# More block products in an attention and token/channel mixer kernel: seven products instead of eight for the first channel product of batches 1 to 3 and for the second of all batches

## The chip, the cores and the metric

The kernel runs on one core of a Trainium2 chip. The metric is the time of one execution on the device in microseconds, the median of the runs of a kernel. Names of engines: PE is the matrix engine (PEld its weight loads), DVE the vector engine, ACT the scalar engine, POOL the general engine, which also issues the casting loads, and SP the engine that issues the other transfers. The kernel's matrix operands are bf16 and its sums fp32.

## The reference

The inputs are q, k and v of 4 batches, 8 heads, 768 positions and 64 channels per head, and four weights of the mixer. Attention keeps 4 sink positions and a window of 128:

```python
scores = scale * np.matmul(q, k.transpose(0, 1, 3, 2))
keep = (pos[None, :] < 4) | ((rel >= 0) & (rel < 128))
a = softmax(np.where(keep, scores, -1e9))
x = np.matmul(a, v)                       # heads side by side: (4, 768, 512)
h = np.maximum(x.T @ w_tok1, 0) @ w_tok2  # over positions, 768 -> 256 -> 768
u = x + h.T
h2 = np.maximum(u @ w_ch1, 0) @ w_ch2     # over channels, 512 -> 1536 -> 512
out = u + h2                              # fp32
```

## The kernel before

One program runs on all engines, with a written order. Heads go in 16 pairs (4 per batch). A pair is loaded as bf16 (`q_bf`, `k_bf`, `v_aug`), q and k are turned (by PE for pairs 0 to 7, by DMA from pair 8 on, `BY_DMA`), the scores of three groups of key tiles (`scores(p, g)`) go into one of two score banks `sc[0]` and `sc[1]`, ACT takes the exponential, DVE or POOL masks it (for the first four pairs PE adds a mask instead, but for one group), PE multiplies by v, and DVE normalizes into `x_sb`. Then come the token product (`mix_h`, `mix_u`), the transpose of u (`uT`), the first channel product with relu (`v1`, into `v1T`), the second channel product, the addition of u (`o_sb`), and the store.

- The first channel product is done in 24 units per batch: for each of 12 tiles of 128 hidden channels and each half of the 768 positions, four matmuls of 384 columns (channel tiles of u), then one eviction with relu on ACT or DVE (L157, L159).
- The second channel product of batches 1 to 3 (`BY_SEVEN = range(1, B)`) is a 2 x 2 block product done with seven products: sums S1 to S4 of blocks of v1T (`add_up`, L1025) and T1 to T4 of w_ch2 (`weight_sums`, L1260), and products accumulated in shared banks, between whose terms a bank is read out by DVE (`evict` in `products`, L1071). Batch 0 does it whole (`whole(st)`, 12 matmuls of 512 columns for each of six row tiles, evicted at L1153).
- [...] Two score tiles take two banks each; four are `mx` banks for all else; behind the first attention, the halves of `sc[1]` are also given out as `mx`.
- The score groups 1 and 2 of pairs 4 to 15 are computed by quarters of 64 rows when they come into `sc[0]`, and by halves when they come into `sc[1]`. Quarters leave out key and query blocks that are masked anyway, and what the bank held there before goes through the exponential and is multiplied by a mask of zeros and ones (L638).

The order of PE's units is the string `ORDERED`. A letter names a stream and a number the unit in it: t, m, s, o, g, h are the first attention and the tokens of batch 0; a the later attention, k the later tokens; c the first channel product; x and y the second one. A planner inside the kernel (`Plan`) walks along this order with costs for each operation and decides which engine does what else, and when. Operations that more than one engine can do go to the one that would end first; the loads are issued on POOL in the order of a list, at most eight outstanding. Each engine then runs its instructions in that order, and each instruction waits for the semaphores of what it needs.

```python
e = min(op.cost, key=lambda e: max(self.free[e], r) + op.cost[e])
```

Of the kernel before, what the change touches and what calls it, by code (L numbers as in the profile page):

```python
# [8 lines left out]

FP32 = mybir.dt.float32  # L10
# [6 lines left out]
def kernel(  # L17
# [43 lines left out]
    BY_SEVEN = range(1, B)  # L61
# [8 lines left out]
    mix_pool = ctx.enter_context(tc.tile_pool(name="mix", bufs=2))  # L70
    v1_pool = ctx.enter_context(tc.tile_pool(name="v1", bufs=1))
# [98 lines left out]
    ones = singles.tile([P, 4 * P], BF16)  # L170
# [11 lines left out]
    mask_main = singles.tile([P, 2, 2, 2, P], BF16)  # L182
    mask_first = singles.tile([P, 2, 2, 2, P], BF16)

    MASKED = -32768.0
    mask_add = singles.tile([P, 4, 2, P], BF16)
# [19 lines left out]
    NKB = 3  # L206
    kTb = [singles.tile([P, S], BF16, name=f"kT{n}") for n in range(NKB)]

# [9 lines left out]
    v_sink_f = singles.tile([P, NHP, 2, D1], FP32)  # L218
# [29 lines left out]
    SEM = 90.0  # L248
    PE_OUT = 190.0
# [10 lines left out]
    class Op:  # L260
        def __init__(self, cost, fn, deps=(), then=(), size=0.0, lag=None, loads=0, traffic=0.0):
# [7 lines left out]
            self.half = False  # L269
# [6 lines left out]
    class Plan:  # L276
        def __init__(self):
            self.free = {"PE": 0.0, "ACT": 0.0, "DVE": 0.0, "SP": 0.0, "POOL": 0.0}
            self.queue, self.landings = 0.0, []
            self.sent = 0.0  # L280
            self.half = False
            self.pending = []
            self.held = [()] * (2 * NSC + NMX)
            self.late = False

        def ready(self, op):
            t = 0.0
            for d in op.deps:
# [3 lines left out]
                t = max(t, d.done)  # L292
# [40 lines left out]
        def other(self):  # L333
            best = None
            queue = False
            for n, op in enumerate(self.pending):
# [6 lines left out]
                if r is not None and len(self.landings) + op.loads > LANES:  # L343
# [11 lines left out]
        def commit_pe(self, op, t):  # L355
# [6 lines left out]
            self.free["PE"] = t + op.cost["PE"] + SWITCH * (op.half != self.half)  # L362
            self.half = op.half
            op.done = self.free["PE"] + PE_OUT + SEM
# [30 lines left out]
    def unit(ns, fn, deps=(), need=None, then=(), half=False):  # L395
# [6 lines left out]
        op.half = half  # L402
        return op

    def burst(*pieces):
# [6 lines left out]
        def run():  # L412
            for p in pieces:
                p.fn()

        op = unit(
            sum(p.size for p in pieces), run, [d for p in pieces for d in p.deps], need,
            [t for p in pieces for t in p.then], half=True,
# [6 lines left out]
    def piece(ns, fn, deps, need, then, keys=()):  # L425
        op = Op({}, fn, deps, then, size=float(ns))
        op.need, op.keys = need, keys
        return op

    def joined(*units):  # L430
# [6 lines left out]
        for u in units:  # L437
# [6 lines left out]
            [t for u in units for t in u.then], half=units[0].half,  # L444
# [4 lines left out]
    def prepare(p):  # L449
# [23 lines left out]
        if p >= BY_DMA:  # L473
# [16 lines left out]
            def sinks_of(e):  # L490
# [5 lines left out]
                {"POOL": 300.0, "DVE": 300.0}, sinks_of, done["kT", p] + [("sk", p - NHP)],  # L496
# [3 lines left out]
        if parts == 2:  # L500
            cost = {"DVE": 540.0, "ACT": 500.0}
        else:
            cost = {"DVE": 950.0} if p < NHP else {"DVE": 950.0, "ACT": 900.0}
# [829 lines left out]
```

## Time and profile before

| | us |
|---|---|
| median of three runs | 205.46 |
| lowest and highest run | 204.59, 206.63 |
| span of the profiled execution, first to last instruction | 203.1 |
| PE busy | 191.1 |
| DVE busy | 130.5 |
| ACT busy | 105.8 |
| POOL busy, with issuing loads | 79.5 |

The profiled execution's own time beside its span isn't given; the median stands 2.4 us above the span. Busy time is the time in which at least one instruction of the engine ran; matmuls overlap, so the time of one matmul is read from the distance of the starts. The granted PE clock is full through nearly all of the span. One row of a timeline gives the start, the time, the engine, the line, the operation, the tile written and the tiles read, their shapes and the number of instructions, and in brackets how long the engine stood idle ahead of it and what ended that.

### The profile page before, as it was taken

Reading aid. Unit: us, or ns where it says so; the run is one execution under the profiler, and the core shown is the slowest. Engines: PE = TensorE matmul, PEld = TensorE weight load, DVE = VectorE, ACT = ScalarE, POOL = GpSimd, SP = SyncE. Lnnn points to the kernel's source line nnn. Section 1 sums busy time; section 2 is a strip of 40 time slices with the busy share of each in tenths; the row PEclk is TensorE's granted clock in tenths of the full one; section 3 lists DMA queues with packets and bytes.
Section 4 is the critical chain, followed back from the end, with each engine's and each line's share of the span. In section 5 each row is a group of like instructions: output and inputs, shape, how many; then the busy total and the mean of one; then the engine's idle time right before and its main releaser. Section 6 shows DMA issues by size and latency. Waiting matters only on the chain.

```text
span 203.1 us, 5055 instructions
## 1 busy us (share of the span) xinstructions
PE 191.1 (94%) x2098; PEld 129.9 (64%) x2107; DVE 130.5 (64%) x272; ACT 105.8 (52%) x189; POOL 79.5 (39%) x121
## 2 busy tenths in 40 slices
PE   6789997999999999999999999999999999999890
PEld 2435685566665564566677788756778886658780
DVE  4657656875978746576677888728657944235851
ACT  4598856878868214396774602677724002673000
POOL 6199869696696563766423050000000000003000
PEclk9999999999999999999999999999999999999997
DMA  5999999999999999999995275500002226100025
GB/s 172 274 283 181 166 185 186 163 170 206 165 152 146 123 184 209 162 157 200 169 131 104 49 87 155 210 0 3 15 14 53 46 62 245 38 0 3 0 101 209
DMA packets 92166, 26.28 MB, mean 129 GB/s; under 512 B 82416, under 2 KB 89072, under 8 KB 92144
## 3 DMA queue, kind: packets, MB, share of 16 engines
q0 software_dynamic: 67232, 11.80, 74.1%
q1 hardware_dynamic: 24912, 14.17, 31.9%
q8 instruction: 16, 0.26, 0.5%
q14 instruction: 6, 0.05, 0.1%
HBM read 26.75 MB, written 6.29 MB: 163 GB/s over the span
## 4 chain that ended last, share of the span: by engine, by line
PE 76%; DMA 9%; POOL 5%; DVE 4%; ACT 2%; issue 1%; SPq 0%; DVEq 0%; POOLq 0%
PE ps_mx L144 62%; PE ps_sc L144 13%; DMA k_bf<-in_k_dram 4%; DMA q_bf<-in_q_dram 3%; DMA v_sink_f<-in_v_dram 2%; POOL v_aug L137 2%; POOL q_bf L129 1%; DVE v1T L1025 1%; DVE o_sb L1071 1%; ACT v1T L157 1%; POOL w_tok L162 1%; PE ps_mx L519 0%; ACT qT L151 0%; DVE x_sb L745 0%; SPq L223 0%
## 5 line engine op out<-in xcount | busy, mean ns | idle before, releaser
L144 PE MATMUL ps_mx<-uT,w_ch 128*128 128x384 bf16 x336 | 60.4, 326 | 0.0
L620 ACT ACTIVATE pT<-ps_sc 128x1024 bf16<-128x1024 f32 (+1 forms) x48 | 44.2, 952 | 25.5 <-PE ps_sc L144 20.0
L144 PEld LDWEIGHTS <-w_ch 128*128 128x128 bf16 x384 | 36.1, 98 | 22.0 <-issue 1.3
L157 ACT ACTIVATE v1T<-ps_mx 128x384 bf16<-128x384 f32 x74 | 36.1, 492 | 26.7 <-PE ps_mx L144 26.3
L144 PEld LDWEIGHTS <-v1T 128*128 128x128 bf16 x288 | 27.5, 98 | 11.0 <-DVE v1T L1025 0.9
L144 PE MATMUL ps_mx<-w_ch,v1T 128*128 128x256 bf16 (+1 forms) x168 | 29.7, 315 | 0.4 <-issue 0.2
L1025 POOL TENSOR_TENSOR v_sums<-v_sums,v1T 128x1152 bf16<-128x1152 bf16 x1 | 2.4, 2367 | 63.7 <-DVE v_sums L1025 63.7
L129 POOL DMA_DIRECT2D k_bf<-in_k_dram x24 | 19.7, 828 | 9.8 <-DMA v_aug<-in_v_dram 6.4
L129 POOL DMA_DIRECT2D q_bf<-in_q_dram x24 | 19.9, 837 | 7.0 <-DMA k_bf<-in_k_dram 2.7
L144 PEld LDWEIGHTS <-w_tok 128*128 128x128 bf16 x192 | 18.3, 98 | 4.7 <-PE ps_mx L144 0.5
L137 POOL DMA_DIRECT2D v_aug<-in_v_dram x16 | 16.9, 1055 | 4.2 <-ACT v1T L157 2.4
L144 PE MATMUL ps_sc<-qT,kT 64*128 64x256 bf16 (+2 forms) x240 | 17.2, 262 | 0.1
L144 PEld LDWEIGHTS <-v_sums 128*128 128x128 bf16 x162 | 15.8, 98 | 2.3 <-issue 0.2
L144 PEld LDWEIGHTS <-pT 128*128 128x128 bf16 x352 | 14.1, 98 | 2.7 <-issue 0.5
L1071 DVE TENSOR_TENSOR o_sb<-ps_mx,u_sb 128x256 f32<-128x256 f32 (+1 forms) x22 | 11.8, 542 | 4.8 <-PE ps_mx L144 4.5
L638 DVE TENSOR_TENSOR pT<-pT,mask_main 128x1024 bf16<-128x1024 bf16 (+1 forms) x22 | 13.2, 630 | 1.0 <-ACT pT L620 1.0
L851 DVE TENSOR_TENSOR u_sb<-ps_mx,x_sb 128x512 bf16<-128x512 f32 x16 | 10.8, 683 | 4.3 <-PE ps_mx L144 4.3
L144 PE MATMUL ps_mx<-q_f,v_sums 128*128 128x256 bf16 x108 | 13.6, 273 | 0.0
L1025 DVE TENSOR_TENSOR v_sums<-v1T 128x1152 bf16<-128x1152 bf16 x6 | 4.5, 757 | 12.8 <-ACT v1T L157 12.8
L144 PEld LDWEIGHTS <-kT 64*128 64x128 bf16 (+1 forms) x240 | 6.0, 99 | 10.5 <-issue 8.0
L144 PE MATMUL ps_mx<-v_aug,pT 128*128 128x65 bf16 x263 | 12.3, 194 | 0.0
L144 PE MATMUL ps_mx<-x_sb,w_tok 128*128 128x256 bf16 x96 | 12.0, 273 | 0.2
(96 smaller groups left out, 248.7 us busy)
## 6 DMA issues: line engine op xcount, KB each, us to landing
v_aug<-in_v_dram POOLq DMA_DIRECT2D x16, 192.0 KB, 8.4
w_ch<-in_moe_w_ch_dram POOLq DMA_DIRECT2D x8, 384.0 KB, 8.7
out_dram<-o_sb SPq DMA_DIRECT2D x12, 256.0 KB, 4.7
out_dram<-o_sb SPq DMA_DIRECT2D x6, 512.0 KB, 2.9
q_bf<-in_q_dram POOLq DMA_DIRECT2D x24, 96.0 KB, 9.0
k_bf<-in_k_dram POOLq DMA_DIRECT2D x24, 96.0 KB, 9.0
q_f<-in_q_dram SPq DMA_DIRECT2D x4, 384.0 KB, 5.7
k_f<-in_k_dram SPq DMA_DIRECT2D x4, 384.0 KB, 6.0
```

The lines of the kernel that those rows point to most:

```text
L129: in_order(nc.gpsimd.dma_start(out=out[:, h], in_=rows[:, h]))
L137: in_order(nc.gpsimd.dma_start(out=v_aug.rearrange("p i t d -> p (i t) d")[:, :, 0:D], in_=v[b].rearrange("h s d -> (h s) d")[2 * hp * S:2 ...
L144: in_order(nc.tensor.matmul(*args, skip_group_check=True, **kwargs))
L157: in_order(nc.scalar.activation(out, in_, AF.Relu))
L162: return in_order(nc.gpsimd.dma_start(out=out, in_=in_))
L620: in_order(nc.scalar.activation(part(tiles["pT", p][:, :, ds(2 * g, 2)]), of_keys(tiles["ps_s", p, g])[:, :, 0:width(g)], AF.Exp, scale=scale,
L638: in_order(nc.vector.tensor_tensor(out=pt, in0=pt, in1=m, op=ALU.mult))
L851: in_order(nc.vector.tensor_tensor(out=u_part(b, g, s0, n), in0=tiles["ps_u", b, g, s0], in1=x_sb[b][:, s0:s0 + n, c0:c0 + cn], op=ALU.add,))
L1025: in_order({"DVE": nc.vector, "POOL": nc.gpsimd}[e].tensor_tensor(out=out(), in0=in0(), in1=in1(), op=how,))
L1071: in_order(nc.vector.tensor_tensor(out=sb(*out), in0=tiles["ps_out", b, t0, key[0]], in1=in1(), op=ALU.add,))
```

## The change

Both channel products are now done as seven block products wherever the diff says so: the second one in all batches, the first one in batches 1 to 3. For the first one, w_ch1 is split in 2 x 2 blocks of hidden channels and of channels, u^T in 2 x 2 blocks of channels and of positions. For each of six hidden tiles f, seven products of two matmuls with 384 columns give the four output blocks. Three of them are kept as fp32 in SBUF (`keep`, two sets of three tiles, `parts`), and three outputs are made on DVE by one instruction that adds the kept part to the bank and clamps at zero (`TENSOR_ADD_SAT`); the fourth is a plain relu. The sums of u^T are made per batch (`first_sums`, four differences of 768 elements per partition), those of w_ch1 once (`first_weight_sums`, eight of 768).

Scores of groups 1 and 2 of pairs 4 to 15 are now computed by quarters in both score banks. The mask is no longer a product with 0 or 1 but a minimum with 0 or 2^127, with one mask row for both heads of a pair (read twice by a stride of zero). The planner's costs are given anew, it counts changes of the matmul's form, and the first and last part of a burst have forms of their own; the order of PE's units is written anew, and so is the order of the loads (`LOADS`). The hidden tile h1T has one buffer instead of two; `ones` and `v_sink_f` lie in tiles that are used later for something else. The order of the two operands of S3 and T3 is exchanged, which changes both signs.

```diff
-        "s11 m10 o5 s12 a0 g1 o6-7 g2 o8 g3-5 h0-1 a1 g6 h2-4 a2 h5-7 c0-1 a3 c2-3 g7 c4-5 a4 c6 a5 c7-11 a6-7 "
...
+        "m10 s11 a1 s12 o5 g1 o6-8 g2-3 h0-1 a2 g4 h2 g5-6 h3-5 a3 h6-7 g7 c16-17 c2 a4 c7 a5-6 c19 c18 c21 a7 "
+        "c13 c9 c5 c10 c22 c6 a8-9 c20 a10 c23 c14 c12 a11 k0 c8 c11 c3 a12 k1 c1 a13 k2 c0 k3 a14 x0 c15 x1 c4 "
...
+        "x26-27 y8 y10 k15 a40-41 y11-12 a42 c66 a43 y13 k16 c67 c69 c80 c73 c68 c81 k17 c71 c82 c74-76 c70 c94 "
...
+        "c145 c139 c138 c146-147 c141 x42 c140 c148 c135 c149 x43 c142 y21 x44 x48 x46-47 x49 y23-24 x45 x52-53 "
+        "x50-51 x54-55 y26 y25 y22 y27"
+    )
+    LOADS = (
+        "t1 v1 q4 v2 k4 v3 t2 q5 k5 v4 c3 c0 k6 q6 c1 k7 c2 v5 q7 d0 d2 v6 q10 q8 k8 d1 v7 d3 k9 q9 k10 v8 "
+        "v13 q14 v9 k11 k12 v10 q11 v15 v12 q13 q12 v14 v11 k13 q15 k15 k14 "
     )
-    BY_SEVEN = range(1, B)
+    BY_SEVEN = range(B)
+    FIRST_BY_SEVEN = range(1, B)
+    HUGE = 3.0e38
...
-            (by_quarters if quarters and tiles["ps_s", p, g] is sc[0] else by_halves)(tiles["ps_s", p, g])
+            (by_quarters if quarters else by_halves)(tiles["ps_s", p, g])
...
-            m = part(mask_first if g == 0 else mask_main)
-            in_order(nc.vector.tensor_tensor(out=pt, in0=pt, in1=m, op=ALU.mult))
+            m = (mask_first if g == 0 else mask_main).rearrange("p k n q -> p (k n q)")[:, 0:width(g)]
+            m = m.rearrange("p (i x) -> p i x", i=1).to_broadcast([P, 2, width(g)])
+            in_order(nc.vector.tensor_tensor(out=pt, in0=pt, in1=m, op=ALU.min))
...
+        def first_sums():
...
+            for name, out, in0, in1, uses in (
+                (1, 0, (0, 1), (0, 0), ()), (3, 2, (1, 1), (0, 1), ()), (2, 1, (1, 1), 0, (1,)), (4, 3, (1, 0), 1, (2,)),
+            ):
+                def run(e, out=out, in0=in0, in1=in1):
+                    in_order({"DVE": nc.vector, "POOL": nc.gpsimd}[e].tensor_tensor(
+                        out=part(out), in0=b_block(*in0), in1=part(in1) if isinstance(in1, int) else b_block(*in1),
+                        op=ALU.subtract,
+                    ))
...
+                    {"DVE": 63.0 + 0.525 * 2 * HS, "POOL": 120.0 + 1.96 * 2 * HS}, run,
...
+        def by_seven(f):
+            slot = parts_used[0] % 2
...
+            def keep(key, n):
+                def run(e):
+                    copy(e, kept[:, n], tiles["ps_f", b, f, key[0]])
...
+                op = Op({"ACT": 382.0, "DVE": 467.0}, run, [last] if last else [])
...
+            def out_of(bank_name, n, i, half):
+                def run(e):
+                    ps = tiles["ps_f", b, f, bank_name]
+                    if n is None:
+                        return relu(e, v1_of(i, half), ps)
+                    in_order(nc.vector._custom_dve(
+                        TENSOR_ADD_SAT, out=v1_of(i, half), in0=ps, in1=kept[:, n], s0=HUGE, s1=0.0,
+                    ))
...
+            banks = {"a": [a1, a6, c22, c12], "c": [c7, c21], "b": [c11]}
...
+            return [
+                product("A11", "B11", "a", a1), product("A12", "B21", "b", c11), product("S2", "T2", "a", a6, a1),
+                product("S3", "T3", "c", c7), product("S1", "T1", "a", c22, a6), product("A22", "T4", "c", c21, c7),
+                product("S4", "B22", "a", c12, c22),
+            ]
...
         for c in range(2):
-            for half in range(2):
-                units += [v1(j * NH + c * KC + n, half) for j in range(2) for n in range(KC)]
+            if b in FIRST_BY_SEVEN:
+                seven = [by_seven(c * KC + n) for n in range(KC)]
+                units += [u for s in seven for u in s]
+            else:
+                for half in range(2):
+                    units += [v1(j * NH + c * KC + n, half) for j in range(2) for n in range(KC)]
...
+    slots = [n for n, op in enumerate(plan.pending) if op.loads]
+    for n, word in zip(slots, LOADS.split()):
+        plan.pending[n] = load_named(word)
```

More of the change, by code (lines that the diff above doesn't have):

```diff
@@ L268, in __init__ @@
             self.need = {}
-            self.half = False
+            self.first = self.last = 0
+            self.after = None
     def landed(at):
@@ L393, in run, with unit @@
                 early -= name not in LATER
-    def unit(ns, fn, deps=(), need=None, then=(), half=False):
+    FULL, HALVES, QUARTERS, EIGHTHS = range(4)
+    def unit(ns, fn, deps=(), need=None, then=(), forms=(FULL, FULL)):
         op = Op({"PE": float(ns)}, fn, deps, then, size=float(ns))
@@ L401, in unit @@
         op.need = need or {}
-        op.half = half
+        op.first, op.last = forms
         return op
@@ L414, in run @@
                 p.fn()
+        changes = sum(p.form != n.form for p, n in zip(pieces, pieces[1:]))
         op = unit(
[L417 to L418 removed]
+            sum(p.size for p in pieces) + SWITCH * changes, run, [d for p in pieces for d in p.deps], need,
+            [t for p in pieces for t in p.then], forms=(pieces[0].form, pieces[-1].form),
         )
@@ L443, in joined @@
             sum(u.size for u in units), run, [d for u in units for d in u.deps], need,
-            [t for u in units for t in u.then], half=units[0].half,
+            [t for u in units for t in u.then],
         )
```

247 lines of the change are left out of this document (183 added, 64 removed), and 17 rows, old and new, of the table ORDERED.

## The prediction

> **What bounds the kernel now.** I read the page first, then the busy time by stretches, then the chain of waits, then single instructions.
>
> ```profile
> span 203.1 us, 5055 instructions
> ...
> PE 191.1 (94%) x2098; PEld 129.9 (64%) x2107; DVE 130.5 (64%) x272; ACT 105.8 (52%) x189; POOL 79.5 (39%) x121
> ...
> DMA  5999999999999999999995275500002226100025
> ```
>
> PE is busy 94% of the span, DVE 64%. The DMA engines are full up to about slice 21, or 107 us. The stretches, with columns length, PE, PEld, DVE, ACT and POOL busy, clock, DMA share, GB/s:
>
> ```profile
> 0.00:10.00 10.00, 7.22 (x67) 3.13 (x67) 5.39 (x24) 4.52 (x7) 3.97 (x12) 1.00 0.95 221
> 10.00:41.00 31.00, 28.06 (x428) 18.38 (x424) 20.93 (x48) 24.20 (x47) 26.45 (x32) 1.00 1.86 194
> 41.00:80.00 39.00, 38.44 (x484) 23.54 (x485) 27.37 (x60) 23.85 (x45) 27.01 (x36) 1.00 1.85 170
> 80.00:130.00 50.00, 49.91 (x544) 34.81 (x543) 36.72 (x71) 26.04 (x43) 19.68 (x43) 1.00 1.28 143
> 130.00:197.60 67.60, 66.88 (x590) 49.73 (x589) 38.98 (x69) 27.21 (x51) 2.37 (x1) 1.00 0.15 46
> 197.60:203.10 5.50, 0.63 (x6) 0.32 (x4) 1.08 (x2) 0.00 (x0) 0.00 (x0) 0.80 0.58 219
> ```
>
> From 41 us on PE has nearly no gap: 0.56 us idle in 41 to 80, 0.09 in 80 to 130, 0.72 behind. Its idle time lies at the start (2.78 + 2.94 = 5.7 us before 41 us) and in the tail (4.9 us of the last 5.5, which are evictions and the store). At the start the chain of waits stands on loads of q and k, for example:
>
> ```profile
> 33.12 7.35 DMA k_bf<-in_k_dram
> ```
>
> So PE work taken out behind 41 us shortens the span one for one, as long as DVE, ACT and the loads keep up.
>
> **The change: PE work removed.** Start to start on PE, for moving tiles of 384, 512 and 256 columns:
>
> ```profile
> 169.91 0.81 PE L144 MATMUL ps_mx<-uT,w_ch 128*128 128x384 bf16 x4
> 170.56 0.81 PE L144 MATMUL ps_sc<-uT,w_ch 128*128 128x384 bf16 x4
> ```
>
> ```profile
> 74.65 0.81 PE L144 MATMUL ps_mx<-w_ch,v1T 128*128 128x512 bf16 x3
> 75.29 0.60 PE L144 MATMUL ps_mx<-h1T,w_tok 128*128 128x256 bf16 x4
> ```
>
> ```profile
> 195.45 0.82 PE L144 MATMUL ps_mx<-q_f,v_sums 128*128 128x256 bf16 x6
> 196.11 2.13 PE L144 MATMUL ps_mx<-w_ch,v_sums 128*128 128x256 bf16 x18
> ```
>
> One matmul takes 0.65/4 = 0.163, 0.64/3 = 0.213 and 0.66/6 = 0.110 us.
> First product, batches 1 to 3: 24 units of 4 matmuls become 6 blocks of 7 products of 2, so 96 become 84: 3 x 12 x 0.163 = 5.9 us less.
> Second product of batch 0: 6 rows of 12 matmuls (72 x 0.213 = 15.3 us) become 7 x 12 + 7 x 6 = 126 of half the columns (13.9 us): 1.4 us less.
> Scores by quarters: from the chain of waits, one pair's three groups of keys:
>
> ```profile
> 101.67 0.32 PE ps_sc L144 x4
> 101.99 1.55 PE ps_mx L144 x34
> 103.54 0.56 PE ps_sc L144 x12
> ```
>
> The first group, by halves, takes 0.32 us (x4), the other two together 0.56, one of them by quarters already (12 matmuls: 4 by halves and 8 by quarters, or the reverse). If a piece by halves takes 0.32, one by quarters takes 0.24. The 12 pieces that stay by halves today save 0 to 0.1 each, 0 to 1.2 in all; I take 0.6, the middle, as some of these pieces are narrower. Sum: 7.9 us.
>
> **What it adds beside PE.** The block products need more evictions: per block three keeps and one relu, which ACT or DVE may take, and three adds that only DVE can do. 24 relus per batch become 24 movable operations and 18 adds. To these come four differences of uT per batch, on DVE or POOL; once, eight sums of w_ch1; and for batch 0 four sums twice and 14 evictions for the 6 of today. Spacing on DVE of an eviction of 384, of a mask, of a sum of 1152 and of an eviction of 512:
>
> ```profile
> 109.50 0.55 DVE L745 TENSOR_TENSOR x_sb<-ps_sc,recip 128x384 bf16<-128x384 f32 x1
> 109.96 0.68 DVE L638 TENSOR_TENSOR pT<-pT,mask_first 128x1024 bf16<-128x1024 bf16 x1
> 110.56 0.68 DVE L851 TENSOR_TENSOR u_sb<-ps_mx,x_sb 128x512 bf16<-128x512 f32 x1
> ```
>
> ```profile
> 112.91 0.76 DVE L1025 TENSOR_TENSOR v1T<-v1T 128x1152 bf16<-128x1152 bf16 x1
> 113.59 0.75 DVE L1025 TENSOR_TENSOR v_sums<-v_sums,v1T 128x1152 bf16<-128x1152 bf16 x1
> ```
>
> ```profile
> 115.86 0.69 DVE L1071 TENSOR_TENSOR o_sb<-ps_mx,u_sb 128x512 f32<-128x512 f32 x1 [0.53 <-PE ps_mx L144]
> 116.47 0.84 DVE L638 TENSOR_TENSOR pT<-pT,mask_main 128x1024 bf16<-128x1024 bf16 x1
> ```
>
> So 0.46, 0.60, 0.68 and 0.61 us. The adding clamp (TENSOR_ADD_SAT) is not in this trace. The nearest row is the eviction of the same 384 elements: 0.46 if it runs at that rate, 0.92 if it needed two passes. I take 0.46, as that row too reads one PSUM and one SBUF operand. The minimum mask has the shape of the product mask, and I take no difference (the masks themselves differ among each other by 0.16 us, 0.68 and 0.84). The sums for batch 0 and for w_ch1 (8 x 0.68 and 8 x 0.45, 9 us, and 14 evictions for 6) lie early, where DVE has 22 of 70 us free (10 to 80 us). A uT difference has 768 of 1152 elements: 0.68 x 768/1152 = 0.45. Per batch that is 18 x 0.46 + 4 x 0.45 = 10.1 us more for DVE.
>
> Does it fit? In 80 to 130 us the relus of v1T number 26, so 1.08 batches (from the view by tile, with ns min/median/max and the first and last start):
>
> ```profile
> L157 ACT ACTIVATE v1T<-ps_mx x19: 491/491/509, 86.6 to 128.3; 128x384 bf16<-128x384 f32 x19
> ...
> L159 DVE TENSOR_SCALAR v1T<-ps_mx x4: 549/557/558, 85.4 to 129.0; 128x384 bf16<-128x384 f32 x4
> L157 ACT ACTIVATE v1T<-ps_sc x2: 491/491/491, 85.5 to 110.9; 128x384 bf16<-128x384 f32 x2
> ...
> L159 DVE TENSOR_SCALAR v1T<-ps_sc x1: 558/558/558, 90.2 to 90.2; 128x384 bf16<-128x384 f32 x1
> ```
>
> DVE there has 36.7 us of work. With 1.08 x 10.1 = 10.9 more, less 2.8 if its five relus go to ACT (26.0 us of 50, so it has room), it has 44.8; PE's work falls to 49.9 - 1.08 x 2.0 = 47.8. DVE goes from 73% to 94% of the stretch that sets the end. On average it fits, and PE stays the bound; in the parts where three adds per block, masks, x_sb and the v_sums fall together it does not, and then a bank is read late and the product queued on it waits. I put 2.5 us for this over the whole run, between 0 (the 9 or so of each 50 us that DVE can still save by running its operations without pauses, since an eviction of 0.55 lets the next start after 0.46) and the price of the first rival below.
>
> POOL is a way out for the sums, with a catch:
>
> ```profile
> 185.85 2.37 POOL L1025 TENSOR_TENSOR v_sums<-v_sums,v1T 128x1152 bf16<-128x1152 bf16 x1 [63.69 <-DVE v_sums L1025]
> ```
>
> ```profile
> 186.55 2.28 DVE L1025 TENSOR_TENSOR v1T<-v1T 128x1152 bf16<-128x1152 bf16 x1
> ```
>
> ```profile
> 116.36 1.71 POOL L631 TENSOR_SCALAR_AFFINE_SELECT pT<-pT 128x256 bf16<-128x256 bf16 x4 [5.62 <-issue]
> ```
>
> The one time that POOL does a sum, the DVE sum beside it takes 2.28 us instead of 0.75; beside four short POOL pieces a DVE mask takes 0.84 (above) instead of 0.68. [...] It speaks against handing the new sums to POOL: if six of them went there, each holding DVE for 1.5 us as here, DVE would lose 9 us and the sum below would come to about 209; by the mask, 0.16 us a time, the loss would be about 1 us. The sum holds nothing of this.
>
> **What it moves.** The written order and the order of loads are new, so every load and every PE unit is at another place. Adding the units' PE times along the order, pair 11's first scores stand behind 73 us of PE work instead of 84, while its q load stands 39th of 49 loads; today the 39th is the k load of pair 12:
>
> ```profile
> 71.51 1.64 POOL L129 DMA_DIRECT2D k_bf<-in_k_dram  x2 [0.56 <-DMA v_aug<-in_v_dram]
> ```
>
> ```profile
> k_bf<-in_k_dram POOLq DMA_DIRECT2D x24, 96.0 KB, 9.0
> ```
>
> ```profile
> kT<-k_bf SPq DMA_TRANSPOSE x8, 8.7
> ```
>
> Landing at 71.5 + 0.8 + 9.0 = 81.3 and turned by DMA in 8.7, plus a second issue, pair 11 is ready at about 91; PE now begins its scores at 101.67 (the row of the scores above) and would be there at 101.7 - 10.5 = 91. No slack is left: 0 to 4 us, and I take 1.0. The first loads (token weights, q of pair 4) come earlier than today, which can remove part of the 5.7 us idle before 41 us, where the chain stands on q and k; the floor of the first 10 us stays. I take 0.8 less, between 2.8 less and 1 more. The end keeps its shape (last product, eviction, store): 0.
>
> **Sum.** 203.1 - 7.9 + 2.5 + 1.0 - 0.8 = 197.9 us of span. The median of the timed runs, 205.46, is 2.4 above the profiled span (they go from 204.59 to 206.63), so the forecast is 200.3 us. By itself this case has 195.5 to 203.4.
>
> **The rivals.**
> (1) DVE takes over as the bound where attention and first product overlap, and the kernel gets slower. The mechanism: DVE runs in program order, an add waits for its product and its kept part, and what is queued behind it (masks, x_sb, u_sb) waits too; then half of its idle time today cannot be filled. In 80 to 130 us DVE would need 36.7 + 10.9 + 13.3/2 = 54.3 us where PE needs 47.8: 6.5 us more, for about two such stretches 13 instead of 2.5, so 200.3 + 10.5 = 210.8. It decides for slower once PE waits over about 8 us more than today. For it: 94% by the count above, three of seven products without a choice of engine. Against: ACT at 52%, and sums that nothing needs at once.
> (2) The loads hold PE: pair 11, and 12 and 13 behind it, come 2 us late each on top, and the front gains nothing: 200.3 + 6 + 0.8 - 1.0 = 206, no clear change. For it: a DMA full to 107 us. Against: PE has channel products to run meanwhile only if the order puts them there.
> (3) DVE hides everything and the new loads clear the front: 203.1 - 7.9 - 2.8 = 192.4, so 194.8. For it: 0.09 us of idle PE in 80 to 130 today. Against: DVE's 94%.
> (4) The block products don't save on PE, because the pause of a bank between its four products (an eviction of 0.55 us after each) shows: 200.3 + 5.9 = 206.2. Three blocks are interleaved in the order, which speaks against it.
>
> **Chances.** Forecast 0.54, (1) 0.27, (2) 0.07, (3) 0.08, (4) 0.04. The likeliest gives the time. The range goes from 195 (just above (3)) to 209.5, which leaves out the upper half of (1). About 1% (2 us) is what a measurement of this kernel can tell from no change: faster means below 203.4, the forecast and (3), 0.62; within 1% the cases (2) and (4), 0.11; slower 0.27.
>
> **What would show it.** Right: PE busy near 183 us in all, first-product matmuls 252 + 96, DVE busy 160 us or more, PE idle between 41 us and the last product 2 to 5 us, most of it behind DVE rows of the adds. Wrong: PE idle there over 8 us (rival 1); waits of PE on kT or qT around 90 to 115 us (rival 2); an add of TENSOR_ADD_SAT over 0.7 us; more than three sums on POOL with DVE rows over 1.5 us beside them.

## The result, and the profile after

The changed kernel takes 214.49 us (median; lowest 213.34) against 205.63 for the kernel before in the same comparison: a ratio of 1.042, with a 95% interval of 1.037 to 1.048. It is slower, and outside the predicted range of 195.0 to 209.5. Ratios here and below leave out executions more than 1.5% above the fastest of their kernel, so they can differ from what the medians, which keep all, would give.

The page of the changed kernel: span, busy time of the engines, and the granted clock in 40 slices.

```profile
span 213.0 us, 5355 instructions
...
PE 187.0 (88%) x2170; PEld 132.6 (62%) x2173; DVE 169.2 (79%) x351; ACT 105.8 (50%) x195; POOL 100.8 (47%) x136
...
PEclk9999999999997599999999999999999999999999
```

PE's busy time fell by 4.1 us, to 187.0, but the span grew by 9.9, so PE stands idle 14.0 us longer. Where, the stretches show (those of the prediction; the last ends with the span):

```profile
0.00:10.00 10.00, 6.79 (x74) 2.75 (x75) 5.63 (x22) 6.10 (x11) 5.30 (x13) 1.00 0.91 217
10.00:41.00 31.00, 27.20 (x445) 18.84 (x447) 22.95 (x59) 22.46 (x41) 26.26 (x32) 1.00 1.84 191
41.00:80.00 39.00, 34.01 (x421) 24.52 (x420) 30.75 (x59) 21.31 (x42) 27.76 (x38) 0.91 1.86 136
80.00:130.00 50.00, 44.82 (x566) 31.65 (x565) 42.54 (x91) 27.05 (x48) 27.45 (x45) 1.00 1.69 138
130.00:197.60 67.60, 62.21 (x566) 44.37 (x565) 57.76 (x107) 28.81 (x55) 14.03 (x11) 1.00 0.22 65
197.60:213.00 15.40, 11.95 (x110) 10.43 (x107) 9.53 (x17) 0.03 (x1) 0.00 (x0) 1.00 0.28 103
```

Idle PE is 7.0 us ahead of 41 us (5.7 before), then 5.0, 5.2 and 5.4 in the three middle stretches, where it was 0.6, 0.1 and 0.7. The long waits among them, from PE's timeline; the bracket names how long PE waited and for whom:

```profile
68.47 1.44 PE L158 MATMUL ps_mx<-q_f,v_sums 128*128 128x256 bf16 x6 [4.86 <-DVE q_f L1418]
...
115.61 0.39 PE L158 MATMUL ps_sc<-qT,kT 64*128 64x256 bf16 x4 [2.74 <-DMA qT<-q_bf]
...
156.62 0.48 PE L158 MATMUL ps_mx<-uT_sums,k_f 128*128 128x384 bf16 x2 [1.59 <-DVE v1T L1107]
...
168.03 1.47 PE L158 MATMUL ps_mx<-q_f,v_sums 128*128 128x256 bf16 x12 [1.46 <-DVE o_sb L1219]
```

The longest is named after DVE, but DVE itself had been waiting. Its timeline and then POOL's:

```profile
66.15 1.80 DVE L1418 TENSOR_TENSOR q_f<-w_ch 128x768 bf16<-128x768 bf16 x1 [4.08 <-DMA w_ch<-in_moe_w_ch_dram]
```

```profile
50.58 0.77 POOL L176 DMA_DIRECT2D w_ch<-in_moe_w_ch_dram  x1
51.31 1.08 POOL L151 DMA_DIRECT2D v_aug<-in_v_dram  x1
52.38 0.76 POOL L176 DMA_DIRECT2D w_ch<-in_moe_w_ch_dram  x1
...
65.18 2.35 POOL L1173 TENSOR_TENSOR v_sums<-v1T,v_sums 128x1152 bf16<-128x1152 bf16 x1
```

The second product of batch 0 now goes by seven, so it needs the sums of w_ch2 (L1418) at once, and the last quarter of w_ch2 is issued at 52.38 and arrives at 66.15: 13.8 us, where a load of w_ch takes 8.2 in the median. The sum behind it takes 1.80 us instead of 0.55 beside a sum on POOL, which belongs to a cause that comes further down; the rest of the wait is the load's.

```profile
w_ch<-in_moe_w_ch_dram POOLq DMA_DIRECT2D x8, 384.0 KB, 8.2
```

In the kernel before, all of w_ch2 was on its way by 44 us, and the sums were wanted a batch later:

```profile
41.03 3.01 POOL L162 DMA_DIRECT2D w_ch<-in_moe_w_ch_dram  x4
```

And the idle time has a price behind it: the slices of the clock show a dip there. The same stretch of the changed kernel by itself, with the granted clock third from the end:

```profile
66.80:73.50 6.70, 5.03 (x37) 3.35 (x37) 6.20 (x9) 1.02 (x1) 4.04 (x7) 0.50 2.83 124
```

At half the clock, 5.03 us of busy PE are some 2.5 us of work (an estimate: half of 5.03). At the full clock PE would be busy 187.0 - 2.5 = 184.5 us. What this is worth in time is not shown: another execution of the same kernel, with a granted clock of 1.000 on the mean, had a span of 212.5 us, only 0.5 less.

### The profile page after: what moved, and what is told of

Same layout as the page of the kernel before. It is cut to its first block, busy times and chain, and to the rows that moved or that the text cites. A ratio compares the mean times of both kernels' runs of the same rounds, so it can differ in the third digit from the quotient of the medians.

```text
span 213.0 us, 5355 instructions
## 1 busy us (share of the span) xinstructions
PE 187.0 (88%) x2170; PEld 132.6 (62%) x2173; DVE 169.2 (79%) x351; ACT 105.8 (50%) x195; POOL 100.8 (47%) x136
## 4 chain that ended last, share of the span: by engine, by line
PE 49%; DMA 23%; DVE 9%; POOL 8%; ACT 5%; issue 4%; SPq 0%; DVEq 0%; POOLq 0%; ACTq 0%
PE ps_mx L158 36%; PE ps_sc L158 12%; DMA w_ch<-in_moe_w_ch_dram 6%; DMA qT<-q_bf 5%; DMA q_bf<-in_q_dram 5%; DMA v_aug<-in_v_dram 4%; POOL k_bf L143 2%; DMA uT_sums<-in_v_dram 2%; DVE v1T L1107 2%; POOL v_aug L151 2%; POOL q_bf L143 2%; ACT pT L640 2%; ACT v1T L171 1%; POOL pT L651 1%; DVE o_sb L1219 1%
## 5 line engine op out<-in xcount | busy, mean ns | idle before, releaser
L158 PE MATMUL ps_mx<-uT,w_ch 128*128 128x384 bf16 x150 | 30.3, 326 | 0.2
L158 PEld LDWEIGHTS <-w_ch 128*128 128x128 bf16 x204 | 19.2, 97 | 13.3 <-issue 3.0
L1107 DVE CUSTOM_DVE_ANT_0 v1T<-ps_mx,parts 128x384 bf16<-128x384 f32 x41 | 21.7, 548 | 4.0 <-PE ps_mx L158 3.8
L165 ACT ACTIVATE parts<-ps_mx 128x384 f32<-128x384 f32 x33 | 15.5, 490 | 17.0 <-PE ps_mx L158 12.2
L158 PEld LDWEIGHTS <-k_f 128*128 128x128 bf16 x144 | 13.6, 97 | 13.3 <-issue 5.6
L171 ACT ACTIVATE v1T<-ps_mx 128x384 bf16<-128x384 f32 x34 | 16.4, 505 | 7.4 <-PE ps_mx L158 7.1
L158 PE MATMUL ps_mx<-uT_sums,k_f 128*128 128x384 bf16 x80 | 17.9, 326 | 1.6 <-DVE v1T L1107 1.6
L158 PE MATMUL ps_sc<-qT,kT 64*64 64x192 bf16 (+3 forms) x288 | 15.3, 251 | 3.1 <-DMA qT<-q_bf 2.7
L1219 DVE TENSOR_TENSOR o_sb<-ps_mx,u_sb 128x512 f32<-128x512 f32 (+1 forms) x30 | 16.2, 549 | 1.4 <-PE ps_mx L158 1.3
L158 PE MATMUL ps_mx<-w_ch,v1T 128*128 128x256 bf16 x126 | 16.4, 273 | 0.0
```

The lines of the kernel that those rows point to most:

```text
L158: in_order(nc.tensor.matmul(*args, skip_group_check=True, **kwargs))
L165: in_order(nc.scalar.activation(out, in_, AF.Copy))
L171: in_order(nc.scalar.activation(out, in_, AF.Relu))
L1107: in_order(nc.vector._custom_dve(TENSOR_ADD_SAT, out=v1_of(i, half), in0=ps, in1=kept[:, n], s0=HUGE, s1=0.0,))
L1219: in_order(nc.vector.tensor_tensor(out=sb(*out), in0=tiles["ps_out", b, t0, key[0]], in1=in1(), op=ALU.add,))
```

## The experiments

Three theories stood at the start. **L**: the new order brings loads too late. **D**: DVE, with 54 adds and more sums, is the bound. **C**: what POOL does beside DVE holds DVE up. Later ones are named where they come up.

### Loads and adds

less_loads gives every other pair from 8 on the q and k tiles of its neighbour, and the same for v:

```diff
+        same = ({9: 8, 11: 10, 12: 13, 15: 14}, {9: 8, 11: 10, 13: 12, 14: 15})[n]
+        if pidx in same:
+            bfs[pidx, n] = bfs[same[pidx], n]
+            return
...
```

> The changed kernel without the q, k and v loads of one pair in two of pairs 8 to 15 (these pairs take their neighbour's tiles, so half of the attention of batches 2 and 3 is computed from other data); order, engines and all else as they were. If late loads are the cause (theory L), most of the 10.2 us that PE idles between 41 and 130 us goes: 214.5 falls to 205 to 208. If DVE is the bound (theory D), the idle time only moves behind other rows and the time stays at 212 to 215.

Measured: 208.38 us, ratio 1.011 (1.002 to 1.020), just above what theory L expected. The waits on qT are gone; 2.89 us behind the w_ch2 sums stay, and so do 1.58 and 1.46 us behind 130 us. So the loads of these pairs are worth some 6 us.

no_adds:

```diff
-                    if n is None:
-                        return relu(e, v1_of(i, half), ps)
-                    in_order(nc.vector._custom_dve(
-                        TENSOR_ADD_SAT, out=v1_of(i, half), in0=ps, in1=kept[:, n], s0=HUGE, s1=0.0,
-                    ))
+                    relu(e, v1_of(i, half), ps)
...
-                op = Op({"DVE": 467.0} if n is not None else {"ACT": 382.0, "DVE": 467.0}, run, deps)
+                op = Op({"ACT": 382.0, "DVE": 467.0}, run, deps)
```

> The changed kernel with the 54 adds of the first product replaced by a relu of the bank that ACT may take too (the kept parts are left out of the result). DVE loses up to 25 us of work. Theory D: the stalls behind 130 us (5.4 us) and part of those before go, 203 to 208. Theory L: only those behind 130 us go, the 10.2 us of idle PE between 41 and 130 us stay, 209 to 212.

Measured: 212.38, ratio 1.033 (1.024 to 1.042): 2 us, though DVE falls from 169.2 to 157.6 us. Both edits together:

> Both of the above at once (half of the loads of pairs 8 to 15 left out, the adds replaced by relus). If loads and adds are all of the loss, the kernel is at PE's own work, 196 to 200. If the two gains overlap (each hides the other's stall), it is near the better of the two single ones; if something else holds PE, above 203.

Measured: 207.06, the median of ten executions from 202.28 to 211.14; the ratio, 0.991 (0.985 to 0.996), rests on the three fastest of them, and the median of all stands 1% above the kernel before. So even with both edits the new form at best comes level with it, and 196 to 200 us are out of reach. In the profiled execution PE still waits 5.87 us behind the w_ch2 sums: that load is not among those left out.

### The late quarter of w_ch2

early_d gives two loads of w_ch2 the places of q10 and q8 in the queue; these, k8 and v7 come behind them:

```diff
+    was = "q10 q8 k8 d1 v7 d3".split()
+    now = [load_named(w).fn for w in "d1 d3 q10 q8 k8 v7".split()]
+    for w, fn in zip(was, now):
+        load_named(w).fn = fn
```

> The changed kernel with two loads of w_ch2 (the second and the last chunk) issued ahead of q10, q8, k8 and v7 instead of among and behind them; the order on every engine is otherwise the same. If the 4.9 us stall of PE at 63 to 68 us is only this load coming late (theory L), the stall goes, and the time falls by 3 to 6 us to 208 to 211; the later stalls on qT stay or grow by up to 2 us. If the DMA engines are simply full (theory B), the stall moves to pair 8 to 10 and the time stays within 1.5 us of 214.5.

Measured: 210.89, ratio 1.023 (1.013 to 1.032), 3.6 us less, and the long wait is short:

```profile
68.10 0.82 PE L158 MATMUL ps_mx<-q_f,v_sums 128*128 128x256 bf16 x6 [1.35 <-DVE q_f L1418]
```

That is two loads out of 49; the last quarter of w_ch2 is issued at 50.47 instead of 52.38. In the four traces that have this exchange, here and below, the wait is 1.76 us at most; in the four that lack it and load all pairs, with POOL at work as in the changed kernel, it is 4.63 to 7.35. Theory L holds for this place.

### Is the order of loads bad as such? Is POOL?

old_loads takes the new list out (the two lines that use `LOADS`, and the list):

> The changed kernel with its new order of PE units but the old order of loads (pair by pair, weights in between). Theory L (the new order of loads is at fault): the late loads go away where PE's order allows, 206 to 212. If PE's new order needs the new loads, PE waits elsewhere: 214 to 222.

Measured: 218.65, ratio 1.065 (1.057 to 1.072). With the new order of PE, the new order of loads is 4 us better than the old one; whether it would do harm with the old order of PE was not run. no_pool takes masks, sums and copies from POOL, by removing "POOL" from their costs:

> The changed kernel with no masks, sums, differences and copies on POOL: DVE (or ACT for the copies) does them, POOL only issues loads and does the early casts. Theory C (POOL's sums and masks block DVE, and hold up the loads queued behind them): faster by 3 to 6 us, 208 to 211. Theory D: DVE gets 15 us more work, slower, 216 to 222. Theory L: the loads come a little earlier, 211 to 215.

Measured: 221.2, ratio 1.080 (1.072 to 1.088), with waits on DVE of up to 4.11 us. That is what theory D said of this run: from 154 to 169 us, ahead of the longest wait, DVE runs with hardly a pause. By this run POOL's help as a whole is needed. But it mixes several things. The two waits of 1.59 and 1.46 us are gone, while copies of key columns now stand on DVE and make it wait twice for 1.88 us ahead of waits of PE of 2.04 and 2.44. I took theory C to have fallen with this run, too early, as the sums show below.

### Mending three load waits at once

loads_mended has early_d's exchange, the second v load ahead of the second token weight, and

```diff
-                {"POOL": 420.0, "DVE": 370.0}, sinks_of, done["kT", p] + [("sk", p - NHP)],
+                {"ACT": 370.0, "DVE": 370.0}, sinks_of, done["kT", p] + [("sk", p - NHP)],
```

> The changed kernel with three edits to its loads: the second batch of v loads goes ahead of the second token weight at the start, the two late w_ch2 loads go ahead of q10, q8, k8 and v7 (as in early_d), and the copies of the sink columns go to ScalarE or VectorE instead of GpSimd, so that no load is queued behind a copy that waits for a transpose. If the loads cost what the named waits say (theory L), PE loses no more to v_aug at 19 us (2 to 3 us and the half clock of 6.8 us behind it, 3.4 us of PE work) and to qT at 96 to 115 us (1.5 to 3.6 us): 204 to 206, PE busy near 184, clock 1.00. If something else takes the place of these waits (DVE, theory D), it stays at 209 to 211.

Measured: 211.23, ratio 1.030 (1.024 to 1.036): no better than early_d. The front is better (PE busy 34.98 of the first 41 us, against 33.99 in the changed kernel), but other load waits come up:

```profile
64.52 0.82 PE L158 MATMUL ps_mx<-q_f,v_sums 128*128 128x256 bf16 x6 [1.76 <-DVE q_f L1418]
...
110.47 0.47 PE L158 MATMUL ps_sc<-qT,kT 64*128 64x256 bf16 x4 [2.02 <-DMA qT<-q_bf]
```

Mending waits one by one does not add up here. That each load moved forward moves another back is my reading; no run shows it for a single load.

### The waits behind 130 us: adds, or sums beside POOL?

Behind 130 us no load is missing, and the two waits of 1.59 and 1.46 us stand in every run so far that has the new order, the adds and POOL's sums. Without the adds the first one goes; without POOL's work both go. What DVE did just before them, in the changed kernel:

```profile
153.34 2.68 DVE L1173 TENSOR_TENSOR v1T<-v1T 128x1152 bf16<-128x1152 bf16 x1
155.95 0.18 DVE L766 RECIPROCAL recip<-ps_mx 128x6 f32<-128x6 f32 x1
...
157.05 0.51 DVE L1107 CUSTOM_DVE_ANT_0 v1T<-ps_mx,parts 128x384 bf16<-128x384 f32 x1
...
164.37 2.67 DVE L1173 TENSOR_TENSOR v1T<-v1T 128x1152 bf16<-128x1152 bf16 x1
166.97 1.01 DVE L1219 TENSOR_TENSOR o_sb<-ps_mx,u_sb 128x256 f32<-128x256 f32 x2
```

and POOL at the same time:

```profile
153.04 2.37 POOL L1173 TENSOR_TENSOR v_sums<-v_sums,v1T 128x1152 bf16<-128x1152 bf16 x1 [10.90 <-DVE v_sums L1173]
155.47 0.92 POOL L167 COPY v_sink<-v_aug 4x65 bf16<-4x65 bf16 x2
156.47 2.36 POOL L1173 TENSOR_TENSOR v_sums<-v1T,v_sums 128x1152 bf16<-128x1152 bf16 x1
164.06 2.36 POOL L1173 TENSOR_TENSOR v_sums<-v_sums,v1T 128x1152 bf16<-128x1152 bf16 x1 [5.23 <-DVE v_sums L1173]
```

A DVE sum that starts just behind a POOL sum takes 2.68 us instead of 0.75 and ends 0.6 us after it; the add at 157.05, with one operand in PSUM, takes 0.51 beside the POOL sum at 156.47. That POOL's sum holds up the DVE sum beside it is theory **K**: with no sum on POOL, the DVE sums should take 0.75 us each, and the two waits should go. sums_on_dve issues the five POOL sums on DVE, at the same places of the program:

```diff
-                    in_order({"DVE": nc.vector, "POOL": nc.gpsimd}[e].tensor_tensor(
+                    in_order(nc.vector.tensor_tensor(
                         out=out(), in0=in0(), in1=in1(), op=how,
```

> The changed kernel with one edit: the sums of v1T that GpSimd makes (five of 1152 columns, 2.36 us each) are issued on VectorE at the same places of the program. In the changed kernel a VectorE sum that reads two SBUF operands beside such a GpSimd sum takes 2.68 us (twice) and 1.80 us instead of 0.75 and 0.55, while the adds beside it, with one operand in PSUM, keep 0.51; the waits of PE of 1.59 us (on v1T) and 1.46 us (on o_sb) stand right behind the two long ones. [...] Theory D (the adds fill VectorE): VectorE gets 3.75 us more work, the waits stay or grow, 214 to 217.

Measured: 213.61, ratio 1.039 (1.034 to 1.044), not clearly less than the changed kernel: 0.9 us by the medians, where the two waits come to 3.05. But the rows show it: each of the eight sums is at 0.75 us at most, both waits are gone, and PE is busy 59.97 of 63 us behind 130 us, where it was busy 57.80 in the changed kernel. The sums, and the two stretches in this order:

```profile
L1173 DVE TENSOR_TENSOR v1T<-v1T x8: 718/748/751, 53.3 to 198.5; 128x1152 bf16<-128x1152 bf16 x8
```

```profile
130.00:193.00 63.00, 59.97 (x551) 43.07 (x550) 54.09 (x108) 27.20 (x52) 4.16 (x7) 1.00 0.24 70
```

```profile
130.00:193.00 63.00, 57.80 (x533) 41.24 (x532) 53.87 (x101) 26.73 (x51) 14.03 (x11) 1.00 0.23 70
```

The wait on w_ch2 was 7.35 us in this trace, which would hide the gain in the time:

```profile
70.77 1.44 PE L158 MATMUL ps_mx<-q_f,v_sums 128*128 128x256 bf16 x6 [7.35 <-DVE q_f L1418]
```

DVE has five sums more to do, though its busy time falls from 169.2 to 166.6 us as none of its sums is held up, and PE waits less: behind 130 us D is wrong. To see K without that load, early_d and loads_mended got the same edit.

> early_d (210.9: two late w_ch2 loads issued ahead of q10, q8, k8 and v7) with the sums on VectorE as in sums_on_dve. There the gain of the sums (the waits of 1.59 and 1.46 us went, all 32 sums at 0.75 us) was hidden by a w_ch2 load that PE waited 7.35 us for instead of 4.86, and by more time at half the clock. With that load early, theory K expects 207 to 209.5; theory D, 211 to 213.

Measured: 207.51, 211.25, 212.13 and 213.07, too far apart for a ratio; the median, 211.69, is where D and not K expected it. PE is busy 59.85 of the 63 us (57.61 in early_d), but a wait on qT of 2.82 us came in at 114 us.

> loads_mended with the sums on VectorE as in sums_on_dve. [...]

Measured: 210.89, ratio 1.018 (1.013 to 1.023, from two executions), with a wait on kT of 2.89 us at 68 us and one of 2.08 on v1T at 94. By the ratio that is 1.2% under loads_mended, by the medians 0.3 us. The gain of 2.2 to 2.4 us of busy PE behind 130 us is in all three traces; ahead of it, the load waits come out differently from kernel to kernel by as much. So these three runs show K in the rows and not clearly in the time. What the adds cost beside that, no_adds_sums tells, with both edits:

> no_adds and sums_on_dve together: the 54 adds are relus that leave the kept part out and may go to ScalarE, and every sum of v1T is VectorE's. From 130 to 193 us PE is busy 57.80 of 63 in the changed kernel, 59.97 with the sums on VectorE, 59.66 without the adds, 62.28 before. If the adds are what is left (theory D's share), PE is busy about 62 there and the time is 209 to 211.5, as the late loads stay. If no_adds only gained because fewer GpSimd sums stood beside VectorE's (GpSimd is busy 6.5 us there instead of 14.0), it stays near 60 and 212 to 214.

Measured: 211.68, ratio 1.029 (1.023 to 1.035); PE is busy 60.44 of the 63 us:

```profile
130.00:193.00 63.00, 60.44 (x575) 43.91 (x572) 47.76 (x95) 33.55 (x70) 4.14 (x6) 1.00 0.25 72
```

The 54 adds cost 0.5 us there, once the sums are out of each other's way; over the whole run the median is 1.9 us under that of sums_on_dve. What is left of the 5.2 idle us, 2.6, is waits of 0.2 to 0.8 us on banks that are still being read and short pauses between units.

### The change's parts in the old order

old_order_new_masks keeps the old order of PE and of the loads, with quarters, minimum masks and the new planner costs; old_order_second adds the second product of batch 0 by seven.

> The old written order and the old order of loads, batches 1 to 3 first product whole and batch 0 second whole, but scores by quarters in both banks, minimum masks and the new costs of the planner. If my 0.6 us for the quarters and nothing for the masks hold: 203.5 to 205.5. If the new costs make the other engines' order worse: 206 to 209.

> As before it, and batch 0 second by seven block products, its 21 units put in the places of the 24 old ones. PE loses another 1.4 us of work, DVE gains 8 us early. If that fits: 202 to 204.5. If w_ch2's sums or DVE hold PE there (as in the changed kernel at 63 us): 206 to 210.

Measured: 211.32, ratio 1.024 (1.015 to 1.034), and 214.95, ratio 1.038 (1.026 to 1.049). Both lie above all that I had expected: 6 us and more from changes that take PE work away. Quarters and masks alone, with the old costs, are quarters_only:

```diff
-            (by_quarters if quarters and tiles["ps_s", p, g] is sc[0] else by_halves)(tiles["ps_s", p, g])
+            (by_quarters if quarters else by_halves)(tiles["ps_s", p, g])
...
-            in_order(nc.vector.tensor_tensor(out=pt, in0=pt, in1=m, op=ALU.mult))
+            in_order(nc.vector.tensor_tensor(out=pt, in0=pt, in1=m, op=ALU.min))
...
-                    out=m[:, i], in0=a, scalar1=-1.0 / MASKED, scalar2=1.0, op0=ALU.mult, op1=ALU.add,
+                    out=m[:, i], in0=a, scalar1=2.0 ** 127 / -MASKED, scalar2=2.0 ** 127, op0=ALU.mult, op1=ALU.add,
```

> The kernel before with two edits only: every scores piece of the later batches goes by quarters, and the masks keep the smaller of value and mask instead of their product. Order of the work, order of loads and the planner's costs stay those of before. The run with the same order but the change's planner costs took 211.3. If the masks and quarters themselves cost (theory M), this run is near 209 to 211 too. If the change's costs and dependences in the planner, which put the operations of the other engines in another sequence, made that run slow (theory S), this one is at 203.5 to 205.5: the pieces by quarters take 0.43 us where halves took 0.56 for two groups, some 1 to 2 us less of PE work, and DVE's idle time is as before.

Measured: 203.94, ratio 0.995 (0.992 to 0.998). They gain 0.9 us, so masks and quarters themselves do not cost (theory M is out), and what else old_order_new_masks holds makes it 7.4 us slower. Theory **S** puts that down to the planner: its new costs put the other engines' work in a worse sequence. One place fits, on DVE and on PE:

```profile
108.06 0.34 DVE L161 COPY kTs<-kT 64x4 bf16<-64x4 bf16 x2 [2.44 <-DMA kT<-k_bf]
108.43 0.56 DVE L763 TENSOR_TENSOR x_sb<-ps_mx,recip 128x384 bf16<-128x384 f32 x1
```

```profile
109.04 1.03 PE L152 MATMUL ps_mx<-h1T,w_tok 128*128 128x256 bf16 x4 [2.25 <-DVE x_sb L763]
```

A copy of four columns, which waits for a DMA transpose, stands on DVE ahead of `x_sb`, and PE waits with it. Of the sixteen copies of this kind 10 stand on DVE in this run and 4 in quarters_only. But this is 2.25 us of the 7.4, and the two kernels differ in more than costs: old_order_new_masks also has the single buffer of h1T, the shared tiles, the one mask row read twice and the planner's new rules. No run takes these one by one. The second product by seven with the old costs and all else as in old_order_second:

> Order of work and loads as before, quarters and minimum masks, the second product of batch 0 by seven block products, first products whole, and the planner's costs those of before. The same with the change's costs took 215.0. By theory S this is 7 or more below: 203 to 207, where the 1.4 us that the second product saves on PE is lost at least in part to the sums of w_ch2, which DVE makes once more and earlier (8 sums of 0.68 us) and which need the last w_ch2 load. By theory M it stays above 211.

Measured: 212.21, ratio 1.035 (1.028 to 1.042), against 1.038 (1.026 to 1.049) with the new costs. This is the one pair of runs that differs in the planner's costs and delays alone, and it shows no difference clear of the noise: S fails as I stated it. The same kind of copy is in the way, under the old costs too:

```profile
79.27 0.34 DVE L160 COPY kTs<-kT 64x4 bf16<-64x4 bf16 x2 [5.52 <-DMA kT<-k_bf]
79.64 0.69 DVE L1212 TENSOR_TENSOR o_sb<-ps_mx,o_sb 128x512 f32<-128x512 f32 x1
```

```profile
80.38 0.82 PE L151 MATMUL ps_mx<-w_ch,v_sums 128*128 128x256 bf16 x6 [3.87 <-DVE o_sb L1212]
```

With batch 3's first product by seven as well:

> As second_old_costs, and the first product of batch 3 by seven block products as well (12 matmuls of 0.163 us fewer on PE, 18 adds and 18 kept parts on DVE and ACT). If DVE has room beside the last batch, this is 1 to 2 us under second_old_costs; if the adds make PE wait as in the changed kernel (rows of 1.5 us at v1T behind 150 us), it is 1 to 3 us above it.

Measured: 214.11, ratio 1.048 (1.042 to 1.053), 1.9 us above it, with four waits of 0.74 to 1.27 us behind 175 us on v1T and on kept parts. And with the copies left to POOL and the sums to DVE:

```diff
-                {"POOL": 300.0, "DVE": 300.0}, sinks_of, done["kT", p] + [("sk", p - NHP)],
+                {"POOL": 300.0}, sinks_of, done["kT", p] + [("sk", p - NHP)],
...
-                    in_order({"DVE": nc.vector, "POOL": nc.gpsimd}[e].tensor_tensor(
+                    in_order(nc.vector.tensor_tensor(
```

> second_old_costs (212.2) with two edits: the copies of the sink columns behind the DMA transposes are GpSimd's alone, and all sums of v1T are VectorE's. In second_old_costs one such copy stood on VectorE ahead of an o_sb addition and waited 5.52 us for a transpose of k that landed at 79.25 us; PE's longest wait, 3.87 us on o_sb, ends there. If that placement is the cost of the second product of batch 0 by seven in the old order, this is 4 to 8 us less: 204 to 208, and with the sums (1.3 us in quarters_sums) perhaps 202.6, where quarters_sums stands. If the seven products themselves cost (more evictions, o_sb in three steps), it stays above 209.

Measured: 207.63, ratio 1.005 (1.000 to 1.011): 4.6 us less for the place of a copy of 0.34 us and for the sums, which were not run apart. The wait at 80 us is gone.

### A version that beats both

quarters_sums is quarters_only with its one POOL sum on DVE.

> quarters_only (203.9) with the one sum that GpSimd makes in it, beside the last batch, on VectorE. The one late wait of PE there, 0.57 us on a sum of v1T at 188 us, stands behind a VectorE sum of 2.28 us beside it. By theory K the wait goes and the time is 0.3 to 0.6 us less: 203.4, below before and after; by theory D no change, 203.9.

Measured: 202.60, ratio 0.988 (0.986 to 0.991): 1.2% under the kernel before, and clear of quarters_only too (0.992 to 0.998). This is where K shows in the time. The sum that took 2.28 us in quarters_only, and the wait of PE behind it,

```profile
185.84 2.28 DVE L1025 TENSOR_TENSOR v1T<-v1T 128x1152 bf16<-128x1152 bf16 x1
```

```profile
188.18 0.83 PE L144 MATMUL ps_sc<-q_f,v1T 128*128 128x256 bf16 x6 [0.57 <-DVE v1T L1025]
```

are a sum of 0.75 us and no wait in quarters_sums:

```profile
184.89 0.75 DVE L1025 TENSOR_TENSOR v1T<-v1T 128x1152 bf16<-128x1152 bf16 x1
```

The time falls by 1.3 us, more than the wait of 0.57; where the rest comes from is not shown. quarters_sums is also 5.0 us under second_kts_sums, which has the quarters and no POOL sum either, but the second product of batch 0 by seven, and the changed kernel's buffers and planner's rules. PE is idle 4.6 us between 41 and 130 us there, and 0.65 here. So no run in the old order gets anything out of the 1.4 us of PE work that the prediction put down for this product.

## Why the prediction was wrong

**PE work removed: nearly right, in part by luck.** 183.2 us of busy PE were forecast; 184.5 are estimated above for the full clock. Quarters were undersized: they take 1.9 us off PE's busy time in quarters_only (191.1 to 189.2), not 0.6. By difference (an estimate) the two block products then took off only 6.6 - 1.9 = 4.7 us, not 7.3, and the two misses nearly cancel. One pair's two groups need 0.42 us instead of 0.56 (an estimate from the starts of two rows, 119.60 and 120.02):

```profile
119.60 0.49 PE L158 MATMUL ps_sc<-qT,kT 64*64 64x192 bf16 x16
120.02 0.40 PE L158 MATMUL ps_mx<-qT,kTs 64*32 64x512 bf16 x4
```

**The add's price: right.** It runs at the rate of an eviction, 548 ns on the mean against 551 for the three relus of the same shape on DVE (L173):

```profile
L1107 DVE CUSTOM_DVE_ANT_0 v1T<-ps_mx,parts 128x384 bf16<-128x384 f32 x41 | 21.7, 548 | 4.0 <-PE ps_mx L158 3.8
```

DVE's 169.2 us are over the 160 given. Rival (1) had the kernel slower, and its sign came: PE is idle far more than 8 us between 41 us and the last product. But its mechanism, DVE as the bound through the adds, is not what happened: without the adds the time falls by only 2 us.

**What it moves: the step that failed.** I priced the new order and the new loads at 1.0 - 0.8 us, by following one pair's q through the queue. It was the wrong row: I never followed w_ch2, though the change makes batch 0 need its sums a batch earlier, and it is w_ch2 that PE waits 4.86 us for (1.25 of it for the POOL sum beside), with 2.5 us more at half the clock behind it. The waits on qT at 96 and 115 us (0.83 and 2.74) came as rival (2) says. The front, where I took 0.8 off, lost 1.3. Together 2.5 + 4.9 + 3.6 + 1.3 = 12.3 us against 0.2 foreseen, of the 15.1 us by which the span, 213.0, misses the forecast of 197.9; PE's work has 1.3 and DVE's waits, less the shorter tail, the last 1.7. less_loads and early_d show that some 6 and 3.6 of the 12.3 can be had back by loads alone; whether the two add up was not run, and for the rest no run has a price.

**POOL's sums: a price that I saw and left out of the sum.** The prediction has the row of a DVE sum beside a POOL sum, 2.28 us instead of 0.75, works out from it what six sums on POOL would cost, and then says that the sum holds nothing of it. Five sums went to POOL. They made three DVE instructions longer by 1.25, 1.93 and 1.92 us, and in the three pairs of traces with and without them, adds kept, PE is busy 2.2 to 2.4 us more behind 130 us without. In this case's rows the sums, with both operands in SBUF, were held up, and the add beside a POOL sum, with one operand in PSUM, kept its 0.51 us; that the place of the operands makes the difference no run shows by itself. The sign I gave for "wrong", more than three sums on POOL with DVE rows of over 1.5 us beside, is what came.

**DVE's waits: near in size, for another reason.** 2.5 us were put down for PE's waits on DVE. The waits named after adds and o_sb come to 0.72, 1.59 and 1.46 us and some of 0.3 to 0.5; the larger two stand behind sums that POOL's held up and go with these. The wait of 1.59 us goes without the adds as well, so it takes both.

**Not foreseen at all.** That one small copy behind a transpose, put on DVE by the planner under the new costs and under the old, can cost PE 2.25 or 3.87 us at one place. This was seen in the old order of PE; in the changed kernel most of these copies are POOL's.

What stays open: why the load waits differ so much between kernels that issue nearly the same loads (1.48 to 3.12 us on qT at 110 to 118 us in seven traces and 0.68 in mended_sums, 4.63 to 7.35 on w_ch2 without the exchange). With the changed kernel's order of loads, PE waits 7.35 us for the sums of w_ch2 in sums_on_dve and not at all in no_pool. So the place in the queue is not all. One trace per kernel was kept, and the executions of one kernel differ by up to 4% (less_and_no_adds), so part of this may be chance from one execution to the next. Open too is how much of the 10 us and more between the mended versions and the forecast is one cause, and what made the old order 7.4 us slower with quarters and the planner's costs, tiles and rules of the changed kernel.

## What to carry to other kernels

When work is moved earlier, list everything that it reads and follow the latest of these through the queue, weights first; one late load of 13.8 us held PE for nearly 5 us, and issuing it and another earlier gave 3.6 us back. A copy of 0.34 us on DVE that waited 2.44 or 5.52 us for a transfer held what stood behind it, and with it PE for 2.25 or 3.87 us, so such a copy belongs on an engine with nothing urgent behind it. And before a sum is handed to the spare engine, look at what the busy one runs at that moment: sums moved back from POOL to DVE made PE wait less (busy 59.97 of 63 us instead of 57.80), though DVE then had more of them to do.

## What was unexpected of the hardware

- **The clock behind a pause.** In the changed kernel the granted clock was 0.50 for 6.7 us, from 1.7 us ahead of the end of a PE pause of 4.86 us to 5.0 us behind it, and in early_d, behind one of 2.97 us, 0.57 over 7.5 us:

```profile
19.50:27.00 7.50, 7.49 (x80) 4.03 (x82) 3.41 (x10) 4.02 (x6) 6.67 (x10) 0.57 1.93 154
```

  Behind 2.02 us in loads_mended it was 0.76 from 110 to 117 us. Behind 2.74 us at 115 us in the changed kernel the clock stayed at 1.00 (115.60 to 122.00 us). So a slower clock followed a pause of 2.02 us here and none a pause of 2.74: the length alone doesn't decide. By the two rows, the slower clock at the pauses of 4.86 and 2.97 us took some 2.5 and 3.2 us of work from PE (estimates: busy time times the missing share of the clock); how much of that reaches the time of the kernel is not shown.
- **Loads beside DMA transposes.** The w_ch load issued at 52.38 us, while SP issued transposes of q and k from 50.83 on, took 13.8 us; the median is 8.2. Whether the transposes slow it is not shown: no run takes them away.
